# Whole loads in place of halved ones, a clearing moved to VectorE, and a new order of the early work in a retention and feed-forward kernel

## The chip, the cores and the metric

The kernel runs on one core of a Trainium2 chip. The core has five engines, each with its own queue of instructions, which it works off strictly in order: TensorE (PE in the profile; PEld are its weight loads) for matrix products, VectorE (DVE), ScalarE (ACT), GpSimd (POOL) and SyncE (SP), which here only issues transfers. An instruction that needs another engine's result waits on a semaphore, and all behind it on the same engine waits with it. Transfers (DMA) run beside the engines on 16 DMA engines, and tell of their landing on semaphores as well. The metric is the time of one execution in microseconds (us), lower is better.

## The reference

```
# q, k, v: (B=4, H=8, S=768, D=64)
gamma = 1.0 - 2.0 ** (-5.0 - np.arange(H))
state = zeros((B, H, D, D))
for t in range(S):
    state = gamma[None, :, None, None] * state + einsum('bhd,bhe->bhde', k[:, :, t], v[:, :, t])
    y[:, :, t] = (1 / sqrt(D)) * einsum('bhd,bhde->bhe', q[:, :, t], state)
x = y.transpose(0, 2, 1, 3).reshape(B, S, H * D)          # (4, 768, 512)
xn = (x - mean(x)) / sqrt(var(x) + 1e-06) * g_ln          # over the last axis
out = x + maximum(xn @ w_ch1, 0.0) @ w_ch2                # w_ch1: 512 x 2048, w_ch2: 2048 x 512
```

## The kernel before, in words

The recurrence over 768 steps is worked in chunks of 128 steps. A *tile* is one chunk of one batch, all eight heads: 24 tiles of 128 rows by 512 columns. Tiles 0 to 3 are the first chunks of the four batches; tiles 4 to 8 are the second to sixth chunk of batch 0, and so on.

For a tile, the first half of the kernel does this. k and q are turned, so that the head dimension lies on the partitions: for tiles 0 to 7 on TensorE (`e_tk`, L504, and `e_tq`, L511), evicted by ScalarE (`trk`) and by VectorE, which multiplies q by its decay (`trq`, L516); for tiles 8 to 23 by a DMA transpose that SyncE issues (`tr`, L526). `pa` (L544) are the products of k and q inside the tile; VectorE multiplies them by a mask with the decay (`asb`, L568). `py` (L592, or L578 from tile 8 on) is `asb` times v, plus q times the state of the chunk before (L588, or L554). The state is summed in `pd` (L651) from k and `vg`, where `vg` (L639) is v times its decay and GpSimd's work, and VectorE puts it into one of two buffers `state` (L665), of which only the blocks on the diagonal are written; the rest is cleared once (`c_zero`, L341). VectorE takes the mean and the variance of the tile (L607, L608) and writes the normalised tile `xn` (L619); ScalarE copies the tile to `x_all` (L625).

The second half is the feed-forward part. `xn` is turned (for tiles 0 to 7 on TensorE, L678, evicted by ScalarE as `xnt`, L256; after that by DMA) and multiplied by w_ch1 (`mm`, L725). Each task is 16 matmuls that fill one bank and need one quarter of w_ch1 (`w1`, quarters 0 to 3); ScalarE, for some tiles VectorE, evicts with a relu to `h1` (L738, L740). The product with w_ch2 (`w2`, four quarters, all needed before the first such product) is L763; VectorE scales it by 1/sqrt(var) and adds `x_all` (L773), and ScalarE issues the store. The square root for that scale is ScalarE's (L700); its function table has to be loaded once, ahead of the first.

GpSimd issues all loads of v, of the weights, and of k and q from tile 1 on, as these are turned from float32 to bfloat16 on their way (L434, L436, L444). For tiles 3, 4 and 5 each load of q, k or v is issued as two of four heads each, as a single packet (`HALVED`, L373, L432 to L435). The transfers of GpSimd's queue take eight semaphores in turn. An issue that takes a semaphore again waits until the transfer that had it last, eight issues earlier, has landed. From tile 8 on (`PACE`) a load also waits behind a small copy (`gate`, L453) that reads the load three before it.

The order of the work is written out: every task is a call of `plan.add` (`a(...)`), with an engine, an estimated time, and what it needs; `ORDER` is a list of task numbers, and `plan.order` only walks that list. So each engine's queue is the list's tasks for that engine, in the list's order (a number of 10000 and more chooses the other engine, one of 100000 and more the other bank). With the estimated times `plan.fill` puts idle-time matmuls on zeros into early gaps of TensorE (L791), until 14 us of its own reckoning.

GpSimd's queue before, from the start, is: two iotas; loads v0, k1, q1, v1, first quarter of w1, k2, q2, second quarter of w1, v2, then k3, q3, v3 as two issues each, third quarter of w1; two memsets of the state; vg of tile 0; k4, q4, v4, k5, q5, v5 as two issues each; fourth quarter of w1, first of w2; k6, q6, k7, q7, v (one more); second quarter of w2; vg of tiles 4 and 5; third and fourth quarter of w2; then the loads from tile 8 on. (k0 and q0 are loaded by SyncE and ScalarE.)

Of the kernel before, what the change touches and what calls it, by code (L numbers as in the profile page):

```python
# [14 lines left out]
PE, ACT, DVE, POOL, SP = range(5)  # L15
# [4 lines left out]
              "k3", "q3", "v3", "w1_2", "k4", "q4", "v4", "k5", "q5", "v5", "w1_3", "w2_0",  # L20
              "k6", "q6", "v6", "k7", "q7", "v7", "w2_1", "w2_2", "w2_3"],
    "bufs": {"qsb": 6, "ksb": 5, "vsb": 9, "qk": 8, "tr": 6, "vg": 3, "trq": 3, "trk": 3},
    "load_pad": 600, "w_pad": 1500, "lead": 32, "lead2": 32, "sq_at": 28000, "late_load": 1700, "two": 4, "m2b": ("b0",), "m2all": 16, "inter": 4, "every": 4, "tail": (0, 384, 512), "step": 8, "pace": 8, "ahead": 3,
    "slack": 600, "tr_pad": 4000, "x_pad": 3500, "vg_pad": 2500, "fill": 0.8, "fill_end": 14000,
}

ORDER = [int(x) for x in """
16 17 2 0 3 19 20 23 14 8 15 1 24 5 7 9 25 4 10 6 21 11 26 18 22 146 45 100147 149 148  # L30
27 150 28 151 153 46 162 100163 29 152 154 164 165 30 155 12 166 31 156 167 32 157 158
159 47 168 176 13 524 169 179 214 100177 170 525 33 215 178 171 172 216 180 34 173 181
532 35 526 36 533 182 37 190 527 534 183 193 38 100191 184 535 48 192 185 186 194 187
195 49 540 542 541 196 204 543 528 197 39 207 100205 198 536 529 40 200 42 43 41 206 544
50 217 234 52 51 53 10537 55 208 100224 54 199 201 545 550 209 225 548 551 210 227 44
226 251 202 549 552 228 218 56 211 546 553 547 222 275 212 219 538 229 235 220 100241
554 539 530 10555 221 213 242 244 531 243 230 231 556 560 57 174 557 258 561 245 261 236
232 233 558 100237 562 238 246 259 247 10559 260 566 563 564 567 262 252 570 203 248 249
254 565 188 255 568 60 250 569 263 100722 160 61 58 59 268 62 287 253 298 63 723 716 724
301 66 264 67 64 717 65 725 269 718 161 571 175 189 719 265 726 266 720 576 100271 270  # L40
276 307 267 578 272 579 577 239 728 273 68 69 278 277 72 729 730 731 318 73 279 70 299
71 280 580 572 732 281 300 282 74 322 284 223 286 734 735 75 288 581 283 285 736 302 303
290 289 573 737 291 738 574 319 584 292 740 741 293 320 294 296 742 308 304 240 585 78
575 743 582 744 295 297 310 333 79 76 309 77 339 586 305 583 311 80 746 587 334 747 312
335 313 314 274 316 323 81 256 315 748 84 350 749 351 588 592 317 325 85 82 83 379 750
589 257 324 354 326 727 602 86 752 87 753 327 328 329 603 593 590 754 755 594 591 330 90
331 340 352 332 342 756 341 343 721 380 598 321 599 595 91 758 336 759 344 760 761 596
733 88 345 89 355 762 346 368 348 353 600 92 757 745 739 337 597 347 93 764 96 349 97 94
381 601 95 765 98 338 357 604 356 766 606 386 99 605 382 607 767 358 306 359 383 614 612
768 360 384 615 361 613 363 770 397 102 771 103 100 362 772 398 365 364 763 369 101 104  # L50
371 370 773 403 610 372 608 774 611 373 776 616 609 399 366 105 374 387 108 109 617 375
618 414 367 377 106 107 777 620 418 751 376 378 389 619 110 388 778 390 779 622 415 391
385 404 780 392 393 621 623 630 782 395 111 114 429 115 631 394 112 400 456 113 433 626
116 624 117 396 406 120 121 416 405 430 783 627 625 407 784 431 408 628 419 409 634 785
410 629 632 411 412 457 118 119 122 413 421 635 786 445 633 420 123 788 126 458 422 127
789 646 124 423 424 790 425 427 647 401 125 426 428 791 642 638 434 436 792 435 794 795
796 639 643 465 769 437 438 640 417 439 440 442 128 797 459 641 129 441 446 443 476 132
644 798 432 402 133 645 636 130 448 447 648 131 134 138 637 460 650 449 450 649 800 651
461 451 452 801 802 477 454 803 444 775 480 462 453 466 478 455 135 491 804 136 137 468
492 467 806 139 495 807 469 470 140 493 808 471 141 809 472 142 474 473 475 652 653 654  # L60
481 483 482 484 810 655 656 658 143 510 479 485 144 787 506 805 657 799 145 659 660 661
486 662 507 496 487 489 664 663 488 508 490 666 498 497 665 499 667 668 670 669 500 671
501 502 672 673 504 511 812 674 503 505 676 513 512 675 514 678 463 677 680 515 679 682
813 681 814 683 516 494 811 509 517 781 519 464 518 520 815 100830 831 816 521 832 818
819 200824 820 825 684 817 793 685 826 690 688 691 827 689 694 696 833 695 522 686 697
687 708 709 821 698 699 692 693 523 822 848 700 828 834 702 100842 701 703 706 707 704
200836 714 837 705 715 712 838 849 843 713 710 711 850 844 845 839 846 851 840 100854
852 855 856 823 847 841 835 829 853 857 860 861 858 862 863 864 859 865
""".split()]


# [90 lines left out]
def kernel(  # L162
# [16 lines left out]
    nc = tc.nc  # L179

    B, H, S, D = q.shape
# [61 lines left out]
    def take(pool, key, shape, dtype):  # L243
        held[pool, key] = pools[pool].tile(shape, dtype, name=pool, tag=pool)
        return held[pool, key]
# [92 lines left out]

    def c_zero(eng):
        for x in state:  # L340
            nc.gpsimd.memset(x, 0.0)  # L341

    a = plan.add
    small = a(DVE, 1200, -100, c_small)
# [11 lines left out]
    qscd = a(ACT, 700, -91, c_qsc, [args, table])  # L356
    maskd = a(DVE, 1230, -50, c_mask, [vscd, tri])
    gchd = a(ACT, 900, 100, c_gch, [small, qscd, vscd], at=9000)
    zerod = a(POOL, 500, 0, c_zero, at=9000)
    exps = [gchd, qscd, vscd]  # L360

    def c_gb(eng):
# [4 lines left out]
        out=grow, in_=moe_g_ln.rearrange("(o n) -> o n", o=1)), lat=2500)  # L367
# [2 lines left out]

    touched = a(SP, 390, -140, lambda eng: nc.sync.dma_start(out=touch, in_=w1_v[:, :, 0:16]), hw=300)

    HALVED = (3, 4, 5)  # L373
    loaded, where, paced = {}, {}, []

    def tile_of(kind, t):
        if kind != "v" and t >= T0:
            return held["qk", t][:, "qk".index(kind)]
        return held[where[kind, t]]

    def load(kind, j, rank):
        takes, uses, follows = None, [], []
        if kind in "qkv":
            b, c = TILES[j]
            src = {"q": q, "k": k, "v": v}[kind][b].rearrange("h (c p) d -> c p h d", p=P)[c]
# [7 lines left out]
            if j == 0 and kind in "kq":  # L393
                raws = []
                for half, eng in ((0, SP), (1, ACT)):
                    hs = slice(half * H // 2, (half + 1) * H // 2)
# [11 lines left out]
                for half, eng in ((0, DVE), (1, ACT)):  # L408
                    if kind == "k":
                        half, eng = None, ACT  # L410

                    def emit(eng, half=half):
                        if not half:
                            take(*takes, [P, H, D], BF16)
                        hs = slice(0, H) if half is None else slice(4 * half, 4 * half + 4)
                        evacuate(eng, held[takes][:, hs],
                                 held["osb", kind].rearrange("p (h d) -> p h d", d=D)[:, hs])
                    parts.append(a(eng, 620 if half is None else 350, -60, emit,
                                   raws + parts[:1], takes if not half else None,
                                   [("osb", kind)] + ([takes] if half else [])))  # L420
                    parts[-1]["after"] = raws[:]
                    parts[-1]["follows"] = parts[:-1]
                    if kind == "k":
                        break
# [3 lines left out]
            def emit(eng):  # L428
                if takes:
                    take(*takes, [P, 2, H, D] if pair else [P, H, D], BF16)  # L430
                dst = tile_of(kind, j)
                if j in HALVED:  # L432
                    for hs in (slice(0, H // 2), slice(H // 2, H)):
                        nc.gpsimd.dma_start(out=dst[:, hs], in_=src[:, hs], single_packet=True)  # L434
                    return  # L435
                nc.gpsimd.dma_start(out=dst, in_=src)  # L436
        else:
            s = slice(j * DM, (j + 1) * DM)
            o = slice(j * KO, (j + 1) * KO)
            src, dst = (w1_v[:, :, s], w1[:, :, s]) if kind == "w1" else (w2_v[:, o, :], w2[:, o, :])  # L440
# [8 lines left out]
        if kind in "qkv" and j >= PACE:  # L449
            old = paced[-AHEAD] if len(paced) >= AHEAD else None  # L450
            if old:
                def gate(eng, old=old):
                    nc.gpsimd.tensor_copy(out=scrap, in_=tile_of(*old)[0:1, 0, 0:1])  # L453
                follows = follows + [a(POOL, 110, rank - 0.5, gate, [loaded[old]],
                                       uses=[where[old]])]
            paced.append((kind, j))
        loaded[kind, j] = a(POOL, ns, rank, emit, (), takes, uses, dma,
                            lat=(LOAD_PAD if kind in "qkv" else W_PAD), follows=follows)

# [10 lines left out]
    for g in range(NG):  # L470
        for ho in range(HO):
            unit["1", g, ho] = u
            u += GROUPS[g] / 4
            every = CFG["every"] if GROUPS[g] == 1 else 8 if 12 <= G0[g] < 16 and GROUPS[g] == 2 else 4
# [17 lines left out]
    for t in range(NT):  # L492
# [138 lines left out]
        if c > 0:  # L631
            for cc in ([0, 1] if c == 1 else [c]):
                if cc == C - 1:
                    continue
                j = number[b, cc]
# [78 lines left out]
    for g in range(NG):  # L714
        n = GROUPS[g]
        hb, h0 = buf_of[g]
        two = GMAX // n
# [109 lines left out]
```

## Time and profile before

| | |
|---|---|
| median of 3 runs | 221.31 us (220.22 to 222.08) |
| the profiled execution's own time | 220.22 us |
| its span, first to last instruction | 218.5 us |
| TensorE busy | 205.9 us, 94% |
| VectorE, ScalarE, GpSimd busy | 121.0, 86.3, 102.3 us |
| mean granted clock of TensorE | 0.982 |
| first matmul of the second layer (L763) | 51.6 us |
| transfers of GpSimd's queue | 13.37 MB written |

All times inside the execution are from the span's start. "Busy" is the time in which an engine works on instructions, without its waits. The granted clock is the share of its full speed at which TensorE was let run. An entry such as `PE mm L725 <- ACT xnt L256` means that the matmuls of line 725, which write `mm`, waited for line 256 on ScalarE, which writes `xnt`; names are without their buffer numbers, so `w` is w1 or w2, and `b` is one of three banks.

### The profile page before, as it was taken

How to read it: one execution, taken by the hardware profiler on the slowest of the kernel's cores; microseconds unless marked ns; L12 is line 12 of the kernel's file. 1: busy time of each engine (PE TensorE's matmuls, PEld its weight loads, DVE VectorE, ACT ScalarE, POOL GpSimd, SP SyncE). 2: the span in 40 equal slices, each digit the busy share in tenths (PEclk: the TensorE clock that was granted, in tenths of full speed). 3: DMA queues.
4: the chain of work that ended last, by engine and by line, in shares of the span. 5: the costliest groups of instructions: out<-in, count | busy, mean ns of one | idle time of the engine just before them, and what ended most of it. 6: DMA issues, size and time to landing. Idle time of an engine off the chain costs nothing.

```text
span 218.5 us, 4950 instructions
## 1 busy us (share of the span) xinstructions
PE 205.9 (94%) x2005; PEld 132.1 (60%) x2027; DVE 121.0 (55%) x260; ACT 86.3 (39%) x175; POOL 102.3 (47%) x160
## 2 busy tenths in 40 slices
PE   7955899999999999999999999999999999999993
PEld 3444799996666666666766766675454444444452
DVE  5753557684547867655785686578785520030041
ACT  5351677765133142424424433353266611444200
POOL 8959998806676795492791585623000000000000
PEclk9995999999999999999999999999999999999999
DMA  9999999999999999999999999998551170000035
GB/s 128 177 181 168 91 124 167 190 195 111 102 114 113 103 154 92 164 199 247 118 127 137 154 157 154 127 117 126 96 170 27 26 218 3 0 0 0 0 141 198
DMA packets 109034, 26.85 MB, mean 123 GB/s; under 512 B 101713, under 2 KB 106065, under 8 KB 109010
## 3 DMA queue, kind: packets, MB, share of 16 engines
q0 software_dynamic: 77168, 13.37, 81.8%
q1 hardware_dynamic: 27186, 6.59, 22.8%
q10 hardware_dynamic: 4656, 6.56, 8.6%
q8 instruction: 16, 0.26, 0.6%
q14 instruction: 8, 0.07, 0.1%
HBM read 27.30 MB, written 6.29 MB: 154 GB/s over the span
## 4 chain that ended last, share of the span: by engine, by line
PE 86%; POOL 4%; DMA 4%; ACT 2%; issue 1%; DVE 1%; POOLq 0%; DVEq 0%
PE mm L725 38%; PE b L763 38%; DMA w<-in_moe_w_ch_dram 4%; PE pd L651 2%; PE pa L544 2%; PE b L578 2%; PE b L554 2%; POOL v L436 1%; POOL k L436 1%; POOL qsb L436 1%; PE b L678 1%; POOL w L444 1%; ACT L700 1%; PE b L592 1%; ACT xnt L256 0%
## 5 line engine op out<-in xcount | busy, mean ns | idle before, releaser
L725 PE MATMUL mm<-xnt,w 128*128 128x128 bf16 (+2 forms) x896 | 96.3, 260 | 0.6 <-ACT xnt L256 0.4
L763 PE MATMUL b<-w,h 128*128 128x512 bf16 (+2 forms) x379 | 88.4, 370 | 1.2 <-issue 0.2
L738 ACT ACTIVATE h<-mm 128x512 bf16<-128x512 f32 x93 | 55.0, 598 | 83.8 <-PE mm L725 83.6
L725 PEld LDWEIGHTS <-w 128*128 128x128 bf16 x896 | 67.2, 99 | 21.2 <-issue 0.8
L763 PEld LDWEIGHTS <-h 128*128 128x128 bf16 x400 | 37.0, 98 | 37.7
L568 DVE TENSOR_TENSOR asb<-pa,mask 128x1024 bf16<-128x1024 f32 x24 | 29.4, 1224 | 18.8 <-PE pa L544 18.4
L773 DVE SCALAR_TENSOR_TENSOR osb<-b,rstd,x_all 128x512 f32<-128x512 f32 (+2 forms) x25 | 18.0, 727 | 27.0 <-PE b L763 26.7
L607 DVE BATCH_NORM_STATS2 bns<-b 128x6 f32<-128x256 f32 (+1 forms) x40 | 17.8, 478 | 18.5 <-PE b L578 11.0
L625 ACT CAST x_all<-b 128x256 bf16<-128x256 f32 (+1 forms) x40 | 16.2, 417 | 23.1 <-DVE xn L619 20.6
L665 DVE TENSOR_TENSOR state<-pd,gch 64x256 bf16<-64x256 f32 x40 | 16.6, 415 | 8.4 <-PE pd L651 7.5
L619 DVE SCALAR_TENSOR_TENSOR xn<-b,mv,gb 128x256 bf16<-128x256 f32 (+1 forms) x40 | 20.1, 533 | 0.8
L639 POOL TENSOR_TENSOR vg<-vsb,vsc 128x512 bf16<-128x512 bf16 x16 | 16.8, 1064 | 4.8 <-PE pd L651 2.8
L436 POOL DMA_DIRECT2D vsb<-in_v_dram x18 | 16.4, 912 | 2.2 <-issue 1.1
L436 POOL DMA_DIRECT2D qk<-in_q_dram x16 | 14.2, 886 | 2.8 <-issue 2.6
L436 POOL DMA_DIRECT2D qk<-in_k_dram x16 | 14.3, 891 | 1.6 <-issue 1.4
L453 POOL COPY scrap<-qk 1x1 bf16<-1x1 bf16 x30 | 5.5, 182 | 16.4 <-DMA qk<-in_k_dram 11.6
L453 POOL COPY scrap<-vsb 1x1 bf16<-1x1 bf16 x15 | 2.8, 186 | 15.2 <-DMA vsb<-in_v_dram 15.1
L706 DVE RECIPROCAL rstd<-rstd 128x1 f32<-128x1 f32 (+2 forms) x14 | 2.0, 157 | 13.4 <-ACT rstd L700 13.4
L533 DVE TENSOR_TENSOR trq<-tr,qsc 128x512 bf16<-128x512 bf16 x16 | 8.0, 500 | 0.1
L791 PE MATMUL pd<-zeros 128*128 128x512 bf16 (+1 forms) x24 | 6.7, 421 | 1.4 <-DVE zeros L291 1.2
L444 POOL DMA_DIRECT2D w<-in_moe_w_ch_dram x8 | 6.5, 831 | 2.9 <-DMA w<-in_moe_w_ch_dram 2.9
L256 ACT COPY xnt<-b 128x512 bf16<-128x512 bf16 x8 | 4.7, 586 | 7.1 <-PE b L678 7.0
(73 smaller groups left out, 137.1 us busy)
## 6 DMA issues: line engine op xcount, KB each, us to landing
out_dram<-osb ACTq DMA_DIRECT2D x23, 256.0 KB, 3.1
w<-in_moe_w_ch_dram POOLq DMA_DIRECT2D x8, 512.0 KB, 8.9
vsb<-in_v_dram POOLq DMA_DIRECT2D x18, 128.0 KB, 4.9
qk<-in_k_dram POOLq DMA_DIRECT2D x16, 128.0 KB, 4.8
qk<-in_q_dram POOLq DMA_DIRECT2D x16, 128.0 KB, 4.8
qsb<-in_q_dram POOLq DMA_DIRECT2D x4, 128.0 KB, 8.0
v<-in_v_dram POOLq DMA_DIRECT2D x3, 128.0 KB, 5.1
qsb<-in_q_dram POOLq DMA_DIRECT2D x6, 64.0 KB, 3.7
```

The source lines that it names most:

```text
L436: nc.gpsimd.dma_start(out=dst, in_=src)
L444: nc.gpsimd.dma_start(out=dst, in_=src)
L568: nc.vector.tensor_tensor(out=take("asb", t, [P, NPAIR, 2, P], BF16).rearrange("p i a t -> p a i t"), in0=held["pa", t], in1=mask.rearrang ...
L607: nc.vector.bn_stats(out=bns[:, t, i, :], in_=x)
L619: nc.vector.scalar_tensor_tensor(out=dst, in0=src, scalar=mv[:, t, 0:1], in1=g, op0=ALU.subtract, op1=ALU.mult)
L625: nc.scalar.copy(out=dst, in_=src)
L639: e.tensor_tensor(out=take("vg", j, [P, H, D], BF16), in0=tile_of("v", j), in1=vsc[:, cc, :].unsqueeze(2).to_broadcast([P, H, D]), op=ALU. ...
L665: nc.vector.tensor_tensor(out=held["pb", n][o, :, o], in0=held["pd", b][o, :, o], in1=gch[o, cc, :].unsqueeze(2).to_broadcast([D, NPAIR, D ...
L725: nc.tensor.matmul(p[:, j, :], lhsT=w1[:, ko, (ho + j) * P:(ho + j + 1) * P], rhs=held["xnt", hb][:, h0:h0 + n, ko, :], start=(ko == 0), s ...
L738: nc.scalar.activation(out=dst, in_=src, func=AF.Relu)
L763: nc.tensor.matmul(held[key][:, 0:w], lhsT=held["h1", hb][:, ho, i * P:(i + 1) * P], rhs=w2[:, ho, cols], start=(ho == 0), stop=(ho == HO ...
L773: nc.vector.scalar_tensor_tensor(out=take("osb", key, [P, w], FP32), in0=held[key][:, 0:w], scalar=rstd[:, t:t + 1], in1=x_all[:, t, cols] ...
```

## The change

Four things are changed.

1. `HALVED` is gone: each load of q, k and v of tiles 3, 4 and 5 is one issue of eight heads, as for all other tiles. GpSimd has nine issues fewer.
2. The two state buffers are cleared by VectorE, and at another place: after `cm` (L327), ahead of its cast of q0. Before, GpSimd cleared them between the third quarter of w1 and vg of tile 0.
3. `w_pad`, the planner's estimate of the time from the end of a weight transfer to its use, is 550 ns in place of 1500.
4. `ORDER` is new in its first third. The matmuls on zeros are the same.

What the new order moves, beside the clearing:

- TensorE: the order is the same up to q of tile 2's transposes (L511). Then came pd of tile 0, xn of tile 1 (L678), pa of tile 2, two w1 tasks, py of tile 2, k of tile 3. Now come xn of tile 1, pa of tile 2, one w1 task, pd of tile 0, py of tile 2, one w1 task, k of tile 3, one w1 task. Then tasks of the same kinds change places until the first L763, which stands after the same number of instructions, 1301, in both; after it py of one tile stands one group of four matmuls later.
- VectorE: `state` of the first chunk moves from before `asb` of tile 2 to behind `asb` of tile 3. Five of the relu evictions are VectorE's in place of three.
- ScalarE: the five exponentials of `gch` (L337) stand before, not behind, the copy `gb` and `trk` of tile 1. The load of the square root's table and the first square root stand right behind `xnt` of tile 0, ahead of `trk` of tile 2; before, they stood some twenty instructions later.
- GpSimd: loads in the same order; one vg later on stands ahead of one load and its gate.
- SyncE: no change.

```diff
-    "load_pad": 600, "w_pad": 1500, "lead": 32, "lead2": 32,
+    "load_pad": 600, "w_pad": 550, "lead": 32, "lead2": 32,
...
 ORDER = [int(x) for x in """
-16 17 2 0 3 19 20 23 14 8 15 1 24 5 7 9 25 4 10 6 21 11 26 18 22 146 45 100147 149 148
-27 150 28 151 153 46 162 100163 29 152 154 164 165 30 155 12 166 31 156 167 32 157 158
+16 17 2 0 3 19 20 23 14 8 15 1 24 5 7 9 25 4 10 6 13 21 11 26 18 45 22 27 146 28 149
+100147 148 150 46 29 151 30 162 100163 153 12 152 165 154 164 166 155 31 156 157 167 32
...
     def c_zero(eng):
         for x in state:
-            nc.gpsimd.memset(x, 0.0)
+            nc.vector.memset(x, 0.0)
...
-    zerod = a(POOL, 500, 0, c_zero, at=9000)
+    zerod = a(DVE, 480, -94, c_zero)
...
-    HALVED = (3, 4, 5)
     loaded, where, paced = {}, {}, []
...
-                dst = tile_of(kind, j)
-                if j in HALVED:
-                    for hs in (slice(0, H // 2), slice(H // 2, H)):
-                        nc.gpsimd.dma_start(out=dst[:, hs], in_=src[:, hs], single_packet=True)
-                    return
-                nc.gpsimd.dma_start(out=dst, in_=src)
+                nc.gpsimd.dma_start(out=tile_of(kind, j), in_=src)
```

## The prediction

> **What bounds the kernel now.** I read the page from the top. Engine shares and slices come first; the columns of the slices are 40 equal parts of 5.46 us.
>
> ```profile
> PE 205.9 (94%) x2005; PEld 132.1 (60%) x2027; DVE 121.0 (55%) x260; ACT 86.3 (39%) x175; POOL 102.3 (47%) x160
> ...
> PE   7955899999999999999999999999999999999993
> ...
> PEclk9995999999999999999999999999999999999999
> DMA  9999999999999999999999999998551170000035
> ```
>
> TensorE is the bound, but for three slices: the third and fourth hold only 5 tenths of PE, and in the fourth the granted clock is half. I leave the rest of the span alone and ask the windows (us, then busy us and instructions of each engine, clock, DMA share, GB/s), cut where the clock changes, and the waits.
>
> ```profile
> 12.62:16.04 3.42, 1.37 (x25) 1.25 (x23) 1.96 (x4) 1.77 (x3) 1.48 (x2) 1.00 1.66 185
> 16.04:19.45 3.41, 0.59 (x6) 0.59 (x6) 0.00 (x0) 0.00 (x0) 3.38 (x5) 0.50 1.96 165
> 19.45:22.87 3.42, 3.29 (x35) 2.92 (x34) 2.07 (x3) 1.01 (x2) 3.42 (x6) 0.50 1.47 148
> 22.87:26.28 3.41, 2.88 (x56) 2.56 (x54) 1.96 (x4) 2.49 (x6) 3.41 (x6) 1.00 1.50 95
> ```
>
> ```profile
> PE pd L651 <- POOL vg L639: 4.9, 1, 4.9
> ```
>
> PE stands from 13.99 to 18.86 us for one product, vg of tile 0, which is GpSimd's. After it the clock is at half until 22.87. In 19.45:22.87 PE is busy all the time and does 35 matmuls, where 22.87:26.28 does 56 with gaps. The chain of waits and GpSimd's timeline say why vg is late:
>
> ```profile
> 7.46 8.32 DMA w<-in_moe_w_ch_dram
> 15.78 0.28 issue
> 16.07 0.74 POOL w L444
> 16.81 0.99 POOL state L341 x2
> 17.80 1.01 POOL vg L639
> 18.82 0.04 issue
> 18.86 0.59 PE pd L651 x4
> ```
>
> ```profile
> 11.81 0.74 POOL L434 DMA_DIRECT2D qsb<-in_q_dram  x1 [0.41 <-DMA w<-in_moe_w_ch_dram]
> 12.71 1.52 POOL L434 DMA_DIRECT2D v<-in_v_dram  x2 [0.16 <-issue]
> 16.07 0.74 POOL L444 DMA_DIRECT2D w<-in_moe_w_ch_dram  x1 [1.84 <-DMA w<-in_moe_w_ch_dram]
> ```
>
> GpSimd's queue issues loads on eight semaphores in turn, so its ninth issue waits until the first has landed, and so on. The six half loads of tile 3 take six of the eight places, and the third w1 quarter (the 16th issue) must wait for the 8th, the second w1 quarter, which lands at 15.78. Behind that issue stand two memsets of the state and then vg.
>
> **The change, part by part.**
>
> *Six issues become three ahead of vg.* The third w1 quarter is now the 13th issue and waits for the 5th, the first w1 quarter: issued 4.98, landing 6.5 later, 11.5 (the wait that ended at 11.81 above). Before it stand v of tile 2 (8.21) and k, q, v of tile 3 at some 0.88 each: GpSimd is there at 8.21 + 4 x 0.88 = 11.7. Then 0.74 for the issue: 12.5.
>
> *The two memsets leave GpSimd* (1.00) for VectorE, right after the causal triangle at 3.39. The zeros' memset, of the same 128x256 words, took 0.27, so 0.54; VectorE stands idle there until 4.58 (a wait of 1.20 for q's landing), so it costs nothing. Without that cover it would cost 0.54. vg thus starts at 12.5, not 17.75, and is done at 13.55, ahead of 13.99.
>
> The Trainium skill, "SBUF — State Buffer", on the trap that VectorE blocks DMA, speaks against this: a VectorE instruction in a two-port mode keeps GpSimd from writing descriptors. The rows: the first issues took 0.89 to 1.01 with VectorE's own memsets and products beside them, later ones 0.87 to 1.04. By the rule up to 0.54 would be added to the first loads; I take nothing.
>
> *What is late next.* With vg gone as a cause, PE goes on at 13.99 with the transposes of xn of tile 1 (xn is done at 13.71 + 0.75 = 14.46), pa of tile 2, and the first product of tile 1 with w1, which needs ScalarE's xnt. On ScalarE a table load (1.28) and a square root (0.29), which stood at 34.99, now follow xnt of tile 0 (ends 12.21). So trk of tile 2 is at 13.78 to 14.36 (it was at 12.91), x_all to 14.95, xnt to 15.6: the product runs from 15.7 to 16.6 (16 matmuls, 0.89), pd to 16.8. Then py of tile 2 needs v of tile 2. This load was issued at 8.21 and landed 10.1 later, at 18.3. What stands ahead of it in the queue is unchanged, so I keep 18.35 and PE waits some 1.55 there. The sqrt is covered by it: asb of tile 2 is done at 16.7; with an earlier v2 the table load would cost up to 1.3.
>
> From there: py 0.23 to 18.7, the product with the second w1 quarter 0.89 to 19.6, and at 19.6 the transposes of k of tile 3 (landed by 18.7). In the kernel before they run at 23.62, after the same matmuls. **Gain at this point: 23.62 - 19.6 = 4.0 us.** It is less than 4.87 for the stall and 2.0 for the half clock (18.86 to 22.87) together, because 1.55 + 0.35 + 0.4 of new waits stand in their place, and a little work is at other places.
>
> *Loads behind vg.* Tiles 4 and 5: twelve half issues from 18.74 to 27.59 (8.85; 1.48 a load) become six at 0.88. They are bound by the queue instead: whole loads that stood behind one another landed some 0.85 apart (k and q of tile 6, issued at 29.06 and 29.93, at 38.7 and 39.5), and w quarters 2.6 apart (issued at 27.59 and 28.32, landed at 35.2 and 37.8). The third w1 quarter still lands at 22.8 (16.07 + 6.7), as data ahead of it is the same. Then 6 x 0.86 = 5.2 to 28.0, the fourth w1 quarter at 30.6 (35.2 before), one w2 quarter 33.2, five loads 37.5, three w2 quarters 45.3 (38.09 + 11.6 = 49.7 before). So these come 4.4 earlier, as much as PE.
>
> *From 19.6 to the first second-layer matmul* (L763, 51.63 before): PE had 27.70 busy in the 28.73 us from 22.87 to 51.60, 1.03 idle. In the new order this can be between 0 (gain 1.0 more) and, if each of the fewer-spaced loads of tiles 4 to 6 is met late, some 2 (1.0 less). By the lines above k4 lands at 23.6, when PE comes to it at about 23.6; w1's fourth quarter at 30.6 against a first use at some 31.4 (37.12 before, less 4.5, and a product and a pa earlier in the new order). Nearly met on all, so I take 0.5 less idle: gain 4.5. That puts L763 at 47.1, w2 at 45.3, slack 1.8 (2.0 now).
>
> *The rest*, 51.60 to 218.50, has 161.94 busy of 166.90. The matmuls and their order are the same but for small swaps; two of the 96 relu evictions go from ScalarE to VectorE (0.60 and 0.69, both beside PE). I take it as unchanged.
>
> **The sum** is against the profiled execution: 220.22 - 4.5 = 215.7. It is the lowest of the three runs; from their median, 221.31, it is 216.8. I say 216.2, between them.
>
> **Rivals.**
>
> *The clock falls all the same, or loads hold PE longer.* Above, the clock fell at 16.04 after a window with 1.37 of 3.42 busy (40%) and 2.05 idle; a window with 2.88 busy kept it. In the window 16.04:19.45 PE would now be busy 0.8 + 1.0 = 1.8, 53%, between the two. If that trips it, 3.41 us at half lose 1.7: gain 2.8, so 217.4 to 218.5. The Trainium skill, "TensorE: Matmul & The Clock Gate", section "HAM oscillation — how this bites in real kernels", says that gaps over some 3.4 us drop the clock; by it the 1.55 wait would not, but here the clock fell 2.05 into a wait, so I do not lean on it. Against the rival: full windows follow.
>
> *Nothing is gained: the w2 wall.* The second layer starts only with all of w2. If the last quarter still lands at 49.7, PE waits 49.7 - 47.1 = 2.6, and with a half clock after it 1.7 more: gain 0.2, 220 to 221. For it: those loads stand in a queue whose landings take 10 to 12 us. Against: GpSimd's issues come over 4 us earlier.
>
> *Slower: the transposed loads late.* Tiles from the ninth on are turned by DMA on SP's queue. The first was issued at 52.19 and took 7.2, 59.4 against its use at 60.96, slack 1.6; the ninth of them at 110.49, took 8.3, 118.8 against 120.10, slack 1.3. If loads in that stage don't come earlier with PE (gated by landings, which took 8 us in places instead of 4), each place waits 4.5 - 1.5 = 3.0 and pays 1.7 of clock: two of them 9.4 against a gain of 4.5: 225. It decides from where the loads come less than 2.4 us earlier at both, as 2 x (4.7 - 2.4) is the gain. Against: GpSimd was waiting for landings that move with the queue.
>
> *The change doesn't do it*: were the third w1 issue still to wait until 15.78, only the memsets' 1.0 would be won and some 0.5 of clock: 219 to 220.
>
> **How the numbers follow.** Forecast, 214.5 to 217.4: 0.58. More gained (v2 early, no gap: 4.87 + 2.0 at most, 213.4 to 214.5): 0.07. Clock or loads, 217.4 to 219.1: 0.18. Nothing, wall or no effect, 219.1 to 223.5: 0.08. Slower, past that: 0.09. The range 214.0 to 219.8 leaves out less than 0.2. About 1% (2.2 us) is what a measurement of this kernel can tell from no change: faster 0.83, same 0.08, slower 0.09.
>
> **What would show it.** Right: vg starts near 12.5, no wait of PE on it; one wait near 16.8 to 18.4 on a v load; a granted clock of 1.0 from the start to the end; first L763 near 47; last w2 quarter near 45.3. Wrong: a half clock in slice four or five, PE waiting in L763 for w2, or DVE's L533 waiting for a transposed load.

## The result, and the profile after

The changed kernel takes 214.63 us (median of four runs, 213.92 to 214.86) against 220.85 us before: a ratio of 0.9706, with a 95% interval of 0.9654 to 0.9759, so 2.9% faster. The forecast was 216.2. The profiled executions took 220.22 and 213.92, so 6.3 us less, where the sum had 4.5; their spans are 218.5 and 212.1.

The page of the changed kernel, engine shares and slices, in the same columns as before:

```profile
PE 204.2 (96%) x2005; PEld 130.8 (62%) x2027; DVE 121.6 (57%) x264; ACT 85.0 (40%) x173; POOL 95.8 (45%) x149
...
PE   7988999999999999999999999999999999999993
...
PEclk9999999999999999999999999999999999999999
DMA  9999999999999999999999999959440260000035
```

The two slices with 5 tenths of PE and the slice at half the clock are gone, and the slice after them holds 9 tenths in place of 8; right of that the rows of PE and of the clock read as before. GpSimd is busy 6.5 us less: nine issues and two memsets. The windows at the same cuts as before:

```profile
12.62:16.04 3.42, 2.93 (x48) 2.59 (x49) 2.79 (x5) 3.04 (x6) 3.04 (x4) 1.00 1.66 185
16.04:19.45 3.41, 3.05 (x59) 2.97 (x57) 2.14 (x5) 1.44 (x3) 2.68 (x4) 1.00 2.04 176
19.45:22.87 3.42, 2.98 (x57) 2.67 (x54) 2.90 (x5) 2.18 (x5) 1.98 (x3) 1.00 1.94 174
```

In these 10.25 us PE does 164 matmuls where it did 66, with the clock at 1.00. In all four executions of the changed kernel the mean granted clock is 0.997 to 1.0. Apart from the 1.2 us at the very start, which both kernels have, PE's waits are now small ones; the one for vg has left the list:

```profile
PE b L498 <- DMA ksb<-in_k_dram: 0.4, 1, 0.4
PE pa L538 <- DVE trq L510: 0.4, 1, 0.4
PE b L586 <- DMA v<-in_v_dram: 0.4, 1, 0.4
PE b L498 <- DMA k<-in_k_dram: 0.3, 1, 0.3
PE mm L719 <- ACT xnt L256: 0.2, 1, 0.2
```

GpSimd's timeline around vg (line numbers are six lower from the loads on):

```profile
10.79 0.98 POOL L430 DMA_DIRECT2D v<-in_v_dram  x1
12.09 0.76 POOL L438 DMA_DIRECT2D w<-in_moe_w_ch_dram  x1 [0.32 <-DMA w<-in_moe_w_ch_dram]
12.85 1.06 POOL L633 TENSOR_TENSOR vg<-v,vsc 128x512 bf16<-128x512 bf16 x1
```

The third w1 issue waits for the first quarter (landed at 11.80) and goes at 12.09, not 16.07; vg starts at 12.85, not 17.75, and is ready when PE comes to it at 16.31. The transposes of k of tile 3 run at 18.18 (23.65 before), the first second-layer matmul at 45.72 (51.63 before), and what follows it takes 166.3 us (166.8 before).

### The profile page after: what moved, and what is told of

Read it like the earlier page. It is cut to its first block, busy times and chain, and to the rows that moved or that the text cites. A ratio compares the mean times of both kernels' runs of the same rounds, so it can differ in the third digit from the quotient of the medians.

```text
span 212.1 us, 4939 instructions
## 1 busy us (share of the span) xinstructions
PE 204.2 (96%) x2005; PEld 130.8 (62%) x2027; DVE 121.6 (57%) x264; ACT 85.0 (40%) x173; POOL 95.8 (45%) x149
## 2 busy tenths in 40 slices
DMA packets 108890, 26.85 MB, mean 127 GB/s; under 512 B 101569, under 2 KB 105921, under 8 KB 108866
## 3 DMA queue, kind: packets, MB, share of 16 engines
HBM read 27.30 MB, written 6.29 MB: 158 GB/s over the span
## 4 chain that ended last, share of the span: by engine, by line
PE 87%; DMA 8%; POOL 3%; issue 1%; DVE 0%; POOLq 0%
PE b L757 39%; PE mm L719 38%; DMA ksb<-in_k_dram 4%; DMA w<-in_moe_w_ch_dram 3%; PE pa L538 2%; PE pd L645 2%; PE b L572 2%; PE b L548 2%; POOL v L430 1%; PE b L498 1%; PE b L672 1%; POOL vg L633 0%; PE b L586 0%; PE b L582 0%; PE b L505 0%
## 5 line engine op out<-in xcount | busy, mean ns | idle before, releaser
L732 ACT ACTIVATE h<-mm 128x512 bf16<-128x512 f32 x91 | 53.8, 599 | 81.4 <-PE mm L719 81.1
L719 PEld LDWEIGHTS <-w 128*128 128x128 bf16 x896 | 66.0, 98 | 20.5 <-issue 0.2
L430 POOL DMA_DIRECT2D vsb<-in_v_dram x20 | 18.0, 901 | 2.7 <-issue 1.6
L447 POOL COPY scrap<-qk 1x1 bf16<-1x1 bf16 x30 | 5.4, 181 | 13.4 <-DMA qk<-in_k_dram 11.7
L572 PEld LDWEIGHTS <-asb 128*128 128x128 bf16 x128 | 5.8, 98 | 2.4
L527 DVE TENSOR_TENSOR trq<-tr,qsc 128x512 bf16<-128x512 bf16 x16 | 6.9, 432 | 0.0
```

Of the source, the lines that this page charges most:

```text
L430: nc.gpsimd.dma_start(out=tile_of(kind, j), in_=src)
L572: nc.tensor.matmul(half_y[h % 2][:, h // 2 * D:(h // 2 + 1) * D], lhsT=held["asb", t][:, h // 2, h % 2, :], rhs=tile_of("v", t)[:, h, :], ...
L719: nc.tensor.matmul(p[:, j, :], lhsT=w1[:, ko, (ho + j) * P:(ho + j + 1) * P], rhs=held["xnt", hb][:, h0:h0 + n, ko, :], start=(ko == 0), s ...
L732: nc.scalar.activation(out=dst, in_=src, func=AF.Relu)
```

## The experiments

The theory to test is called *places* in the expectations: halves use up the eight semaphore places of GpSimd's turn, the third w1 issue then waits for the second quarter, vg behind it is late, PE stands, and its clock falls. The rivals put the gain down to the order, to the memsets, or to the longer issuing of the halves.

**The parts of the change, one by one.** First, only the halves go:

```diff
-    HALVED = (3, 4, 5)
+    HALVED = ()
```

> The kernel before with whole loads of tiles 3 to 5, nothing else: the clearing stays on GpSimd and the old order stays. Theory (places): the halves hold six of the eight places in GpSimd's turn of semaphores, so with whole loads the third w1 issue goes at some 12.1 and vg of tile 0 starts 1.0 after it is issued, at 13.85 (two memsets between), 3.9 us earlier than 17.75; PE waits about 1.0 for it, the clock stays at 1.0, k of tile 3 is turned near 18.3 and the time is 214.5 to 216. Rival (order): the new order is what pays, and in the old one the freed time is lost in other waits: 217.5 to 219.5. Rival (clearing): the two memsets are what holds vg: no more than 1 us gained.

Measured: 215.34 us against 221.40 for the kernel before in the same series, ratio 0.978 (0.9696 to 0.9865), as *places* had it. vg starts at 13.39, PE waits 0.7 for it, k of tile 3 is turned at 17.89, the first second-layer matmul runs at 46.0.

```profile
PE mm L725 <- ACT xnt L256: 0.7, 2, 0.4
PE pd L651 <- POOL vg L639: 0.7, 1, 0.7
```

So the whole loads bring most of the gain by themselves, in the old order and with the memsets where they were (by the interval, between 1.4% and 3.0%). The rivals "order" and "clearing" fall as main causes.

Then only the clearing is moved:

```diff
-    zerod = a(POOL, 500, 0, c_zero, at=9000)
+    zerod = a(DVE, 480, -94, c_zero)
...
-            nc.gpsimd.memset(x, 0.0)
+            nc.vector.memset(x, 0.0)
```

(and task 13 stands in `ORDER` where the changed kernel has it).

> The kernel before with only the clearing of the state on VectorE, at the place of the changed kernel; halved loads and old order stay. Theory (places): vg starts 1.0 earlier, 16.8, PE still waits 3.9 us and the clock still falls: 0.5 to 1.5 us gained, 219 to 220. Rival (clearing): the memsets hold GpSimd up for more than their 1.0, and 3 us or more are gained.

Measured: 219.99 us, ratio 0.9937 (0.9901 to 0.9973). PE still waits for vg, and the clock still falls, in the profile and in all but one of the other nine executions. vg comes 0.75 after the third w1 issue in place of 1.68, but starts at 17.69, not at the 16.8 expected, as the second w1 quarter landed only at 16.65 in this execution (15.78 in the profile before).

```profile
PE pd L651 <- POOL vg L639: 4.0, 1, 4.0
```

Both together in the old order, against the changed kernel, leave the order (the memsets' own line and task 13 stand as in the run before):

```diff
-    HALVED = (3, 4, 5)
+    HALVED = ()
...
-    zerod = a(POOL, 500, 0, c_zero, at=9000)
+    zerod = a(DVE, 480, -94, c_zero)
```

> The changed kernel's whole loads and its clearing on VectorE, in the old order (and the old planning constant, which moves nothing by itself): against the changed kernel it shows the order alone. Theory (places): vg starts at 12.85, no wait for it; the order is worth less than 1 us: 214 to 215.6. Rival (order): 217 or more, since in the old order ScalarE's table load stands at 35 us and the products of tile 1 come behind pd.

Measured: 215.46 us, ratio 0.9754 (0.9696 to 0.9812). vg starts at 13.46 (12.85 expected; the first w1 quarter landed at 12.41 here), and PE doesn't wait for it. Moving the memsets adds nothing that can be measured once the loads are whole: they are 1.0 us of GpSimd's time ahead of a product that is then nearly in time. To size the order, the changed kernel (no edit) and this one were run again in one series:

> The changed kernel as it is, in one series with the next, which differs from it in the order alone. From the runs so far (214.63 and 215.46, medians of four) the order is worth 0.8; the theory holds if the two stand 0.3 to 1.3 apart in this series too, the order being the smallest part of the change.

> Whole loads and the clearing on VectorE in the order of the kernel before, once more, in one series with the changed kernel. Theory: 215.0 to 216, 0.3 to 1.3 above it. Rival (the order is worth nothing): within 0.3 of it.

Measured: 214.22 us (213.68 to 214.79, ratio 0.9708, 0.9665 to 0.975) and 215.13 us (214.4 to 216.3, ratio 0.9748, 0.9705 to 0.9791). So the order is worth 0.9 us within this series, and 0.8 between the first two medians (214.63 and 215.46), which come from different series. The two intervals overlap, so the size is uncertain. In the second pair of profiles the first second-layer matmul stands at 45.98 and 46.29.

**Halves back in the changed kernel.**

```diff
-                nc.gpsimd.dma_start(out=tile_of(kind, j), in_=src)
+                dst = tile_of(kind, j)
+                if j in HALVED:
+                    for hs in (slice(0, H // 2), slice(H // 2, H)):
+                        nc.gpsimd.dma_start(out=dst[:, hs], in_=src[:, hs], single_packet=True)
+                    return
+                nc.gpsimd.dma_start(out=dst, in_=src)
```

> The changed kernel with the halved loads of tiles 3 to 5 put back. Theory (places): the third w1 issue waits again until 16.1, vg (no memsets ahead of it) runs 16.8 to 17.9; the new order puts xn, pa and a product ahead of pd, so PE waits 1.5 us for vg, not 4.9, and the clock may stay; then the loads of tiles 4 and 5, at 1.5 us each from 17.9 on, bring the fourth w1 quarter to 34 where PE wants it near 32, so 1.5 to 2.5 more: 217 to 218.5. Rival (order): the order alone pays, and the time is within 1 us of the changed kernel, 214.6.

Measured: 218.47 us, ratio 0.9896 (0.9825 to 0.9967): 3.8 us given back, though the order is the new one. The third w1 issue goes at 16.13 again and vg starts at 16.89. PE's waits, and the windows (us, busy us and matmuls of PE first) around the longer one:

```profile
PE mm L725 <- DMA w<-in_moe_w_ch_dram: 2.3, 1, 2.3
PE pd L651 <- POOL vg L639: 1.3, 1, 1.3
```

```profile
26.82:30.24 3.42, 3.42 (x68) 3.21 (x66) 1.77 (x3) 2.64 (x7) 3.42 (x6) 1.00 1.18 101
30.24:33.65 3.41, 1.09 (x23) 0.91 (x19) 2.17 (x6) 0.60 (x1) 3.41 (x5) 1.00 1.14 178
33.65:37.07 3.42, 3.40 (x34) 3.01 (x35) 0.40 (x1) 1.07 (x2) 2.92 (x4) 0.50 1.90 165
```

The new order softens the wait for vg to 1.3, but the fourth w1 quarter lands at 33.62, 3.8 us later than in the changed kernel, and PE stands for it; in this profile the clock falls there instead. This is a second hurdle that the kernel before had hidden behind the first. Of the four executions two have a mean clock of 0.992 (218.60 and 219.91 us) and two of 0.999 and 1.0 (218.33 and 217.53), so the loss does not hang on the clock.

**Which halves?**

```diff
-    HALVED = (3, 4, 5)
+    HALVED = (3,)
```

> The kernel before with only tile 3's loads in halves; tiles 4 and 5 are whole. Theory (places): the six halves ahead of the third w1 issue are what makes it wait for the second quarter, so vg still starts near 17.7, PE waits some 4.8 us, the clock still falls, and at most 1 us is gained: 220 to 221.4. Rival (issue time): the halves cost by the longer issues of all three tiles, mostly those of tiles 4 and 5, and 3 us or more are gained: 218 or less.

Measured: 221.64 us, ratio 1.0028 (0.9999 to 1.0056). vg starts at 18.08, PE waits 4.9 and the clock falls: nothing is gained, although the last w2 quarter lands at 46.84, 2.8 earlier than before. The wait is as *places* had it, and the time 0.2 above its range; early loads are no use to a late PE.

The other way round:

```diff
-    HALVED = (3, 4, 5)
+    HALVED = (4, 5)
```

> The kernel before with only the loads of tiles 4 and 5 in halves; tile 3's are whole. Theory (places): vg starts near 13.5, PE waits 0.7 us, the clock stays; the twelve halves leave GpSimd by 24 and the queue is still nearly full, so the fourth w1 quarter lands at 31 to 32 where PE wants it near 31.5: 215 to 216.5, most of the gain. Rival (issue time): 218 or more, with PE waiting 2 us or more for that quarter.

Measured: 219.59 us, ratio 0.9913 (0.9878 to 0.9948). My number was a miss by 3 us, and the rival's was right. In the profile vg of tile 0 is early (14.53) and the clock stays, as the theory says, but PE then waits 2.7 at 32 to 34.6 for vg of tile 4, a wait that neither theory named. (In five of the nine executions the mean clock is 0.988 to 0.992, so there it did fall for a while; these took 218.98 to 219.96 us, the four at 1.0 took 218.09 to 219.64.) PE's wait, and GpSimd's timeline ahead of it:

```profile
34.62 0.38 PE L651 MATMUL pd<-vg,ksb 128*128 128x128 bf16 x4 [2.66 <-POOL vg L639]
```

```profile
23.02 0.74 POOL L434 DMA_DIRECT2D ksb<-in_k_dram  x1 [1.82 <-DMA w<-in_moe_w_ch_dram]
23.92 1.49 POOL L434 DMA_DIRECT2D qsb<-in_q_dram  x2 [0.16 <-issue]
25.39 1.50 POOL L434 DMA_DIRECT2D vsb<-in_v_dram  x2
26.85 1.52 POOL L444 DMA_DIRECT2D w<-in_moe_w_ch_dram  x2
...
33.41 2.15 POOL L639 TENSOR_TENSOR vg<-vsb,vsc 128x512 bf16<-128x512 bf16 x2
```

GpSimd leaves vg of tile 0 at 15.5 and the twelve halves at 26.85: 11.3 us for what took 6.4 as six whole loads in the changed kernel (13.84 to 20.25), because each costs at least 0.74 and the eighth of them again hits the eight places (1.82 until the third w1 quarter landed). Everything behind them in its queue is late by that: the fourth w1 quarter (33.0), the last w2 quarter (48.66), and vg of tiles 4 and 5. So the longer issuing matters as well, but only once vg of tile 0 is out of the way.

**vg ahead of the waiting issue**, all halves kept (task 214 is vg of tile 0, 47 the third w1 load):

```diff
-159 47 168 176 13 524 169 179 214 100177 170
+159 214 47 168 176 13 524 169 179 100177 170
```

> The kernel before, all halves kept, with vg of tile 0 issued by GpSimd ahead of the third w1 load instead of behind it and the memsets. Theory (places): vg runs 14.2 to 15.3, PE waits 1.3 and the clock stays, k of tile 3 is turned near 18.7; the memsets end at 17.8, so the loads of tiles 4 and 5 go only 1 us earlier, the fourth w1 quarter lands near 34 and PE waits some 2 for it, as with the halves put back into the changed kernel: 217.5 to 219. Rival (only the clock and the wait count): no such second wait, and 215 to 216.5.

Measured: 219.56 us, ratio 0.9912 (0.9879 to 0.9946), 0.6 above the expected span. vg runs from 14.30 to 15.35. In the profile PE does not wait for it at all, but it comes late to it, at 16.70: its clock reached full speed only at 13.55 here (5.8 in the profile before). PE's only wait for a vg is the later one of tile 4, and then it waits 0.9 for k of tile 6:

```profile
16.70 0.39 PE L651 MATMUL pd<-vg,k 128*128 128x128 bf16 x4
...
34.49 0.38 PE L651 MATMUL pd<-vg,ksb 128*128 128x128 bf16 x4 [0.97 <-POOL vg L639]
...
38.03 0.40 PE L504 MATMUL b<-idn,ksb 128*128 128x128 bf16 x4 [0.93 <-DMA ksb<-in_k_dram]
```

Had PE come at 13.99, as in the profile before, it would have waited some 1.4 (15.35 - 13.99, an estimate). So moving one instruction, with the same loads, takes most or all of the wait away, which shows what the wait was. The clock does not fall after that here, and the mean granted clock is 0.997 or more in six of the other eight executions. That only 1.7 us come of it fits the second hurdle: both later waits are for GpSimd's work or loads behind the halves. The wait for the fourth w1 quarter that I had expected is not in this list; the wait for vg of tile 4 stands ahead of it. The first second-layer matmul runs at 50.33. The profile is one execution, with a late start of the clock; the time is that of nine.

**The clock alone.** TensorE fills its wait with matmuls on zeros; vg is as late as ever:

```diff
         for t in plan.fill(plan.order(ORDER), PE, 1100, FILL_END, FILL, warm):
+            if t is plan.tasks[215]:
+                warm(4600)
             t["emit"](t["eng"])
```

> The kernel before with 4.6 us of matmuls on zeros on TensorE in its wait for vg (they feed nothing); vg is as late as before. It measures the clock by itself. Theory (the half clock cost up to 2.0 of the gain): the clock stays at 1.0, pd runs at 18.9 as before, k of tile 3 is turned near 22 in place of 23.65, and 1.2 to 2 us are gained: 219.4 to 220.2. Rival (loads hold PE anyway): what is won goes into waits for the loads of tiles 4 and 5, and the time is within 0.5 us of the kernel before.

Measured: 218.99 us, ratio 0.992 (0.9877 to 0.9962): 0.8 to 2.7 us gained; the median is 0.4 below the expected span. The clock stays at 1.00 throughout those windows, pd starts at 19.04 (18.86 before), its wait filled, and k of tile 3 is turned at 22.34 in place of 23.65. vg came 0.2 later here (17.94), so by the profiles the half clock cost 1.3 to 1.5 of the early loss, not 2.0, and the rest was the wait.

**The packet option**, left out with the halves kept:

```diff
-                        nc.gpsimd.dma_start(out=dst[:, hs], in_=src[:, hs], single_packet=True)
+                        nc.gpsimd.dma_start(out=dst[:, hs], in_=src[:, hs])
```

> The kernel before with its halves, but each half without the single-packet option. Theory (places): it is the number of issues that costs, the option changes nothing: vg starts at 17.7 to 18.1, twelve halves of tiles 4 and 5 take 8.8 to 9.2 us of GpSimd, and the time is within 1 us of the kernel before, 220.3 to 222.3. Rival (the option costs): each half takes clearly less than 0.74 us to issue or lands sooner, and 2 us or more are gained.

Measured: 220.14 us, against 220.80 for the kernel before in the same series, ratio 0.9984 (0.995 to 1.0018). vg starts at 17.53, and the twelve halves take GpSimd from 18.52 to 27.37, 8.85, as before. The option does nothing that can be measured; the number of issues does.

**The runs side by side.** The times are from the profiled executions' traces. The last column is the span less the start of the first second-layer matmul (L763).

| kernel | ratio | PE's wait for vg of tile 0 | last w2 quarter lands | L763 starts | after that |
|---|---|---|---|---|---|
| before | 1 | 4.9, clock falls | 49.66 | 51.63 | 166.8 |
| tile 3 halved | 1.0028 | 4.9, clock falls | 46.84 | 52.61 | 167.0 |
| clearing on VectorE | 0.9937 | 4.0, clock falls | 49.33 | 52.24 | 166.9 |
| wait filled | 0.9920 | filled, 0.1 | 49.87 | 51.07 | 166.1 |
| vg first | 0.9912 | none (PE late) | 48.74 | 50.33 | 166.6 |
| tiles 4, 5 halved | 0.9913 | 0.7 | 48.66 | 49.89 | 166.8 |
| changed, halves back | 0.9896 | 1.3 | 48.31 | 50.36 | 166.4 |
| whole loads | 0.9780 | 0.7 | 44.49 | 46.00 | 166.9 |
| changed | 0.9706 | none | 44.24 | 45.72 | 166.3 |

Two things hold PE ahead of L763: the late vg of tile 0, with which L763 stands at 51 to 53, and what comes late behind the halves of tiles 4 and 5 in GpSimd's queue (the fourth w1 quarter, vg of tile 4, k of tile 6), with which it stands at some 50. Opening only one leaves the other: 0 or 1.7 us. Opening both gives 6. The work after L763 takes the same time in all, to within 0.9.

## Why the prediction was right

The mechanism held as predicted, step by step, and one size was off. The median, 214.63, lies 1.6 below the forecast and only 0.6 inside the lower end of the range, and the gain between the profiled executions was 6.3 us, not 4.5. What came is close to the case of an early v of tile 2, which the prediction put at 213.4 to 214.5 and gave 0.07.

- *The third w1 issue as the 13th, waiting for the first quarter*: 11.7 and done at 12.5 in the sum, 12.09 and 12.85 measured, as that quarter landed at 11.80 and not 11.5. vg at 12.85 instead of 12.5. Right. The first quarter's landing varies: 11.2 to 12.6 over the 13 profiles.
- *The memsets*: two on VectorE, from 3.38, 0.55 together, ahead of a cast that waits till 4.70. Free, as said. The issue beside them, from 3.24, took 0.89, as it did before without them, so nothing of the trap that the Trainium skill's "SBUF — State Buffer" (section "SBUF: two separate sides") tells of can be seen here, for a memset of this size. For this chip that page does not name a memset among the operations that contend (section "Who interferes with whom"), so the prediction's 0.54 "by the rule" does not follow from it.
- *v of tile 2 at 18.35*: **the term that was mis-sized.** It landed at 17.01, and PE waited 0.36 where I had 1.55. That is 1.2 of the 1.4 us by which this landmark was missed (k of tile 3 at 18.18; 19.6 in the sum), and two thirds of the 1.8 by which the sum was short. I took the landing from the one execution that I had, on the ground that what stands ahead in the queue is unchanged. The queue is; the landing was an exception. In the other twelve profiles, halved or whole, this load lands 0.89 to 0.97 after the second w1 quarter; in the profile shown of before it landed 2.57 after it. In the trace's semaphore updates 15 of the 16 DMA engines had finished it by 16.43, and one came at 18.35.
- *Table load and square root covered*: ScalarE's xnt of tile 1 came at 14.78, PE waited 0.2 for it. v of tile 2 came later than all that. Right, with less cover left than the sum had.
- *Loads 4.4 earlier*: the fourth w1 quarter at 29.81 (30.6 in the sum), the last w2 quarter at 44.24 (45.3): 5.4 earlier. The third quarter landed at 22.18 in place of 22.8. The spacings held on average: 0.91 and 0.85 for the two runs of loads of q, k and v (0.85 in the sum), 2.2 to 2.6 for the w quarters (2.6).
- *From k of tile 3 to L763, 0.5 less idle*: 27.54 us, where it was 27.98. Right.
- *The rest unchanged*: 166.3 against 166.8, within the 166.1 to 167.1 of all profiles. Right.

Of the rivals, the fallen clock did not come: the window of 16.04:19.45 had 3.05 of 3.41 busy, since PE waited less than I thought. The w2 wall did not come either: L763 stood 1.5 behind the last w2 quarter, where I had 1.8, and no profile shows PE waiting in L763 for w2. In the three kernels with halves in tiles 4 and 5 and a nearly open vg, w2 is late as well (48.3 to 48.7), but PE was held earlier, by other work behind the same halves and, in the one with vg first, also by the late start of its clock; L763 came at 49.9 to 50.4, with times of 218.5 to 219.6. The transposed loads of the slower rival moved with the rest: the first was used at 54.44, 1.96 after its landing (1.6 before). The halves' part in the loss was not only the place they took ahead of vg; I had both parts in the sum, but not that either alone would leave most of the time where it was.

## What to carry to other kernels

When a queue of transfers takes its semaphores in turn, count issues, not bytes: splitting one load in two may put an unrelated issue, and the compute behind it in that engine's queue, behind a transfer that nobody needs yet. Look for the second hurdle before pricing the first: here the waits behind one hurdle hid those behind the other, and the sum of the single removals (0 and 1.7 us) says nothing of removing both (6). And a single landing time from one execution is a sample; the spacing between neighbours in the queue is what repeats.

## What the runs showed of the hardware

- From one change of TensorE's clock to the next it took 10.24 and 6.82 us in the kernel before, 27.30 and 3.41 with the halves back in the changed kernel: whole multiples of some 3.41. So a profile can be cut into windows of that length at its changes of the clock. The clock fell after windows with PE busy 1.37 us (40%; before) and 1.09 (32%; halves back), and, in the other three profiles in which it fell ahead of the end, after 0.83, 0.80 and 0.00 us. It stayed after one with 1.81 of 3.42 (53%; tiles 4 and 5 halved), though PE's single wait there was 2.7 us, longer than the 2.3 that came before the fall with the halves back: the 2.7 us straddled two windows. The way back is not the same: with the clearing on VectorE a window at half the clock with 1.89 busy (55%) was followed by another at half. So the share of one window fits where the length of a wait does not. The clock fell 2.05 us into the wait in the kernel before and at the end of 2.3 us with the halves back, sooner than after the 3.4 us of idle time that the Trainium skill's "TensorE: Matmul & The Clock Gate" (section "HAM oscillation — how this bites in real kernels") gives; the measurement decides.

```profile
30.14:33.56 3.42, 1.81 (x39) 1.63 (x37) 1.81 (x4) 2.67 (x5) 3.42 (x5) 1.00 1.21 190
33.56:36.97 3.41, 2.35 (x43) 2.35 (x43) 1.82 (x3) 0.93 (x3) 2.74 (x4) 1.00 1.85 170
```

- When the clock first rises varies: between 3.9 and 7.2 us in twelve of the 13 profiles, 13.55 in one, with the same matmuls on zeros ahead of it. Why it was so late there is open.
- GpSimd took 0.74 to 0.84 us to issue a load of 64 KB (512 rows of 128 bytes) and 0.87 to 1.04 for one of 128 KB, in the kernel before: the cost is mostly per issue. Why one DMA engine was 1.9 us late with v of tile 2 in one execution was not settled.
